# RWKV-7 recurrence feeding a merged four-expert MLP: the order of TensorE's products in a pass, rearranged from the sixth pass on

## The chip, the cores and the metric

The kernel runs on one core of a Trainium2 chip, in fp32. The metric is the device time of one execution in microseconds (us), lower is better; the median of a few executions is compared. Engines are named as in the profile: PE is TensorE's matrix products and PEld its weight loads, DVE is VectorE, ACT is ScalarE, POOL is GpSimd, SP is the engine that issues most DMAs. Each engine works through its own instructions in their order; semaphores connect them.

## The reference

Two stages. The first is a linear recurrence over 768 tokens for 4 x 8 heads of 40 channels. The second takes the 3072 tokens with 320 channels through four experts of hidden size 1024, weighted by normalised domain probabilities.

```python
for t in range(S):                                   # B, H, S, D = 4, 8, 768, 40
    y[:, :, t] = einsum('bhd,bhde->bhe', r_t, state)
    Sa = einsum('bhde,bhe->bhd', state, a_t)
    state = state * w_t[:, :, None, :] - einsum('bhd,bhe->bhde', Sa, b_t) \
            + einsum('bhd,bhe->bhde', v_t, k_t)
x = y.transpose(0, 2, 1, 3).reshape(3072, 320)
p = domain_probs / (domain_probs.sum(-1, keepdims=True) + 1e-9)
for e in range(4):
    out += p[:, e:e+1] * (maximum(x @ w1[e], 0) @ w2[e])
```

## The kernel before, in words

**Units and passes.** Tokens are cut into 12 chunks of 64. A *unit* is one chunk of two batches (128 partitions are 2 x 64 tokens); there are 24 units (`NU`). The main loop (line 1100) has one *pass* per unit u = 1 to 23 and weaves four kinds of work into it: the state step of unit u and u+1 (`step`), the inverse of unit u+1 (`merge`), the work inside unit u+2 and u+3 that needs no state (`within`, `substitute`), and the MLP of chunks already finished (`todo`). All but the MLP are generators; `run(gen, n)` lets n of their parts emit instructions, so the loop's order of calls is the order in which work is emitted. `EARLY` is 5: passes below 5 have one order, the others another. Unit 0 and 1 go through the MLP one by one (`mixture_of_unit`), later units two at a time (`mixture_of_chunk`).

**Two forms of product.** Everything with heads of 40 channels uses a quarter of the array: products of 64 rows by 64 columns (`quadrants`, line 383), four at a time in the four quadrants. The MLP and the transposes use the full 128 x 128. In between stands one case: the input has 320 = 128 + 128 + 64 channels. The first MLP product of a weight piece therefore has a part on the *last* 64 channels, in quadrants (`up_last`, line 751), and a *main* part on 256 channels, in the full form (`up_main`, line 765); both add into the same two PSUM banks (`ph`), the last channels first. I call a run of quadrant products between full ones a *quadrant stretch*, and the other a *full stretch*.

**MLP pieces.** `ups(e, x)` makes half the hidden layer of expert e: last channels, main part, relu on ACT (line 778) into `hs`. `down_1` is one tile of three products of 8 steps (`p431`, 12 matmuls in the program), `down_2` two tiles (`p75`, `p26`, 16 matmuls); they take `w2`, sums of it, and sums of `hs` (`a`, DVE, line 897). Their results are scaled and added into `osb` on DVE (line 791; the first expert's line 789). Half of these adds are 320 wide, half 160. In the trace each such fp32 matmul appears twice: 12 in the program are 24 rows. `piece.lead` emits only the part on the last channels, ahead of its piece, so that it falls in a quadrant stretch. `mix(n)` emits n pieces; a pass takes 8 (two in each `gap`), of which four are ups. `w1` pieces (640 KB) arrive in two buffers, `w1p`; the next load waits until the piece before the last has been used.

**State step.** `step` has for each unit: `prn` (state times A, and the transposed state), RH on DVE (line 654), SN on ACT; `psat`, then SaT and SX copies on ACT; `pxr`, from which DVE makes the masked part of SX (line 400) and ACT the copies RS (line 700); `pdy`, a K term and an N term per quadrant; then Y and the new state on DVE, and Y goes by DMA into xT. The N term needs SX.

**Work inside a unit.** `within`: G (scan of decays, DVE), `pg` (transpose of G, PE), gp (product and reciprocal, DVE), n_tok, k_tok, AT (DVE), VT and RT (32 x 32 transposes on DVE of raw loads), `pNT`, `pKT` (transposes, PE) and copies NT, KT (ACT); `pc` and VC (masked copy, DVE); `pfe` and F (ACT); `pe` and ET (masked copy, DVE); `pev` and EV (ACT). `substitute` inverts the triangular F: blocks (DVE and ACT), M (DVE, line 553) and a long run of small operations on POOL giving Z. `merge`: Qc and QTc (transposes on DVE, lines 604 and 606), `pY`, Yq (ACT), `pQ`, QT (ACT).

**What sets the order.** A scheduler orders the instructions of an engine by its own estimates, except where `tc.keep_in_program_order` pins them. `in_order[0]` pins all products on TensorE; it is on up to u = 5 and off after it. `pin` pins some of `within` for the first units. `q.apart` is set for units from `EARLY + 2`: F is copied before `pe` is made. PSUM has 8 banks: 5 (`big`) for the recurrence, used in turn, 3 (`mm`) for the MLP. A tile that takes over a bank waits until the old contents have been read.

Of the kernel before, what the change touches and what calls it, by code (L numbers as in the profile page):

```python
# [15 lines left out]
def kernel(  # L16
# [42 lines left out]
    P = 128  # L59
# [342 lines left out]
    def within(q):  # L402
# [74 lines left out]
        if q.u > 1:  # L477
            pin(turn_raw(q.AT[:], n["rawA"][:]))
        at_ij = q.AT[:].rearrange("p (i j) t -> p i j t", i=2)
        ins = other.tensor_tensor(out=at_ij, in0=at_ij, in1=Gv.rearrange("p (j i) t -> p i j t", i=2), op=ALU.mult)  # L480
        pin(ins)
# [13 lines left out]
        if q.u == 1 or q.u >= PADDED:  # L495
            causal_scores(VT)
            yield
# [10 lines left out]
        if q.apart:  # L508
            copy_F()
            yield  # L510
# [125 lines left out]
    def step(q, xT):  # L636
# [59 lines left out]
        if not q.start:  # L696
# [10 lines left out]
        pdy = quadrants(  # L707
            banks("pdy"), 0, BY_TOKENS, D + L - lo,
            lambda j, s, i: (i, s, j, q.K[half(i), head(j, s), :], q.VC[half(i), head(j, s), lo:D + L]),
            lambda j, s, i: (i, s, j, q.N[half(i), head(j, s), :], SX[half(i), head(j, s), lo:D + L]),  # L710
        )
# [39 lines left out]
    def up_last(k, xT, n):  # L751

        w1 = pieces[k]
        ph = [ps.tile([P, HF // 2, n], FP32, name="ph", tag="mm", bufs=3) for _ in range(2)]

        for f in range(HF // 2):
            for c in range(2):
                for i in range(2):
                    matmul(
                        out=ph[i][half(c), f, :], lhsT=w1.last[part(i), f, half(c)],  # L760
                        rhs=xT[part(i), 2, :], start=(f == 0), stop=False,
                    )
        return ph

    def up_main(k, xT, n, ph):

        w1 = pieces[k]
        h = sb.tile([P, HF, 2 * P], FP32, name="hs", tag="hs", bufs=3)
        for i in range(2):
            for f in range(HF // 2):  # L770
                for g in range(2):
                    at = i * HF // 2 + f
                    matmul(
                        out=ph[i][:, f, :], lhsT=w1.main[:, g, at * P:(at + 1) * P],
                        rhs=xT[:, g, :], start=False, stop=(g == 1 and f == HF // 2 - 1),
                    )
        for i in range(2):
            nc.scalar.activation(  # L778
                out=h[:, i * HF // 2:(i + 1) * HF // 2, 0:n], in_=ph[i][:], func=ACTF.Relu,
            )  # L780
        return h

# [18 lines left out]
    def mixture_of_unit(q):  # L801
# [3 lines left out]
        def ups(e):  # L805
            ph = []

            def lead():
                if not ph:
                    ph.append(up_last(at + 2 * e, q.xT, P))  # L810

            def piece():
                lead()
                hs[e] = [up_main(at + 2 * e, q.xT, P, ph[0])]
                hs[e].append(up_main(at + 2 * e + 1, q.xT, P, up_last(at + 2 * e + 1, q.xT, P)))
                used(at + 2 * e + 2)
                if q.u == 0 and e + 2 < E:
                    load_w2(e + 2)

            piece.lead = lead  # L820
            return piece
# [44 lines left out]
    def mixture_of_chunk(qs, xT):  # L866
# [4 lines left out]
        def ups(e, x):  # L871
            k, ph = at + 2 * e + x, []

            def lead():
                if not ph:
                    ph.append(up_last(k, xT, 2 * P))

            def piece():
                lead()
                hs[e, x] = up_main(k, xT, 2 * P, ph[0])  # L880
                used(k + 1)

            piece.lead = lead
            return piece
# [96 lines left out]
    def lead():  # L981
        if todo and hasattr(todo[0], "lead"):
            todo[0].lead()

# [115 lines left out]
    for u in range(1, NU):  # L1100
        in_order[0] = u <= EARLY
# [16 lines left out]
        ahead = u + 3 < NU and u in range(EARLY, EARLY + 3)  # L1118
        if ahead:
            go(load_raw(begin(u + 3), "W"))  # L1120
        if early:
            lead()
        run(w_next, 99 if early else 1)
        run(s, 1)
        gap(0)


        if early:
            run(s, 1)
        run(w, 1)  # L1130
        if not early:
            run(w_next)
            run(s)

        if early:
            run(w, 1)
            gap(1, 2 if u + 1 == EARLY else None)
            run(s)
        if u == 1:
            mixture_of_unit(q)  # L1140
        elif q.bp:
            mixture_of_chunk(units[u - 1:u + 1], chunks_x[q.c])
        if not early:
            begin_later(len(later))
            run(w, 1)
            run(m, 1)
            gap(1)

        if u + 3 < NU:
            go(load_raw(units[u + 3] if ahead else begin(u + 3), "A" if ahead else "WA"))  # L1150
            load(units[u + 3], "WBKV")
            later.extend(load_raw(units[u + 3], "VR"))
        run(w, 2)

        soon = u in (2, 3, 4)
        if soon:
            run(w, 1)
        if early:
            run(m, 1)
        else:  # L1160
            run(s_next, 1)
            run(m, 1)
        if soon:
            substitute(units[u + 2], nc.gpsimd)
        gap(2)

        if not early:
            run(m, 1)
        if not soon:
            run(w, 1)  # L1170
        if not early:
            lead()
            run(s_next, 1)
        if not soon and u + 2 < NU:
            substitute(units[u + 2], nc.gpsimd)
        if early:
            run(w, 1)
        if u + 3 < NU:
            ws.append(within(units[u + 3]))
            run(ws[u + 3], 1)  # L1180
        if early:
# [5 lines left out]
        else:  # L1187
            gap(3)
        s = s_next
    mix(len(todo))  # L1190
# [30 lines left out]
```

## Time and profile before

| | |
|---|---|
| median of 3 runs | 1103.84 us (1103.26 to 1104.54) |
| the profiled execution, its own time | 1102.3 us |
| its span, first to last instruction | 1100.6 us |
| mean granted TensorE clock | 0.991 |
| DMA moved | 122.18 MB, mean 111 GB/s |
| DVE, ACT, POOL busy, 246.33 to 932.28 us | 498.88, 230.03, 348.26 of 685.95 us |

The stretch from 246.33 to 932.28 us holds passes 6 to 21, which repeat; before it lie the first units, after it the last two units and the rest of the MLP. Busy times of PE are modelled from starts, and products overlap, so an idle time of PE is shown only where a gap is longer than a product; the starts in the timeline tell more. A line's times are the start, the length, and at the end, in brackets, the idle time of the engine before it and what ended it. "x32" is how many instructions were merged into the row.

### The profile page before, as it was taken

To read this page: it belongs to the slowest core of one execution; us is meant where nothing else is said; L and a number is where in the kernel's file an instruction comes from. 1 tells how busy PE (TensorE), PEld (TensorE's weight loads), DVE (VectorE), ACT (ScalarE), POOL (GpSimd) and SP (SyncE) were. 2 spreads that over 40 slices of the span, in tenths; PEclk is the share of its full clock that TensorE was granted. 3 is DMA by queue.
4 is the path that set the end of the run, shared out by engine and by line. 5 is a ranking of instruction groups with operands and counts; after the bars stand their busy time and mean duration, and the time that the engine had idled before them with its cause. 6 is when DMAs were issued, how large, how long until landed. Compare 5 with 4: busy or idle time off the path is not lost.

```text
span 1100.6 us, 38528 instructions
## 1 busy us (share of the span) xinstructions
PE 1070.0 (97%) x16102; PEld 955.8 (87%) x16102; DVE 756.6 (69%) x1551; ACT 353.0 (32%) x956; POOL 502.9 (46%) x1274
## 2 busy tenths in 40 slices
PE   6799899999999999999999999999999999999998
PEld 6677788789998999898999989989998989988887
DVE  7766668887777776767767768767767677543343
ACT  2432444223233233243233242332332432321110
POOL 5106677753463653743734635636537437430000
PEclk9799999999999999999999999999999999999999
DMA  7776545425345363354353444443552532222320
GB/s 117 226 247 138 136 103 117 119 55 136 98 111 127 98 140 97 94 146 103 93 144 94 102 121 104 116 120 84 127 123 65 147 85 67 98 69 82 104 76 13
DMA packets 268868, 122.18 MB, mean 111 GB/s; under 512 B 213736, under 2 KB 242072, under 8 KB 268696
## 3 DMA queue, kind: packets, MB, share of 16 engines
q1 hardware_dynamic: 265416, 119.12, 43.0%
q8 instruction: 127, 2.08, 0.8%
q10 hardware_dynamic: 3280, 0.61, 0.3%
q14 instruction: 45, 0.37, 0.1%
HBM read 111.79 MB, written 3.93 MB: 105 GB/s over the span
## 4 chain that ended last, share of the span: by engine, by line
PE 81%; DVE 7%; POOL 5%; ACT 3%; issue 2%; DMA 1%; SPq 0%; ACTq 0%; DVEq 0%; POOLq 0%
PE ph L76 35%; PE p L76 28%; POOL Z L593 3%; PE pdy L76 3%; PE psat L76 2%; PE pxr L76 2%; POOL Z L580 2%; PE prn L76 1%; PE pfe L76 1%; PE pQ L76 1%; PE po L76 1%; PE pc L76 1%; DVE Z L590 1%; PE pY L76 1%; DVE M L553 1%
## 5 line engine op out<-in xcount | busy, mean ns | idle before, releaser
L76 PE MATMUL ph<-xT,w1p 128*128 128x256 f32 (+3 forms) x3040 | 446.3, 377 | 4.0 <-issue 3.9
L76 PEld LDWEIGHTS ph<-xT,w1p 64*64 64x64 f32 (+1 forms) x3040 | 338.5, 162 | 72.7 <-issue 29.0
L593 POOL TENSOR_TENSOR Z<-Z 128x31 f32<-128x31 f32 (+7 forms) x704 | 260.0, 369 | 55.2
L897 DVE TENSOR_TENSOR a<-hs 128x512 f32<-128x512 f32 x220 | 151.8, 707 | 104.7 <-ACT hs L778 104.7
L580 POOL TENSOR_TENSOR Z<-M,Z 128x62 f32<-128x62 f32 (+7 forms) x352 | 144.1, 409 | 132.3 <-DVE M L569 106.4
L778 ACT ACTIVATE hs<-ph 128x512 f32<-128x512 f32 (+1 forms) x208 | 115.3, 564 | 226.5 <-PE ph L76 225.4
L76 PE MATMUL p<-sums,a 128*128 128x160 f32 x1056 | 164.9, 299 | 0.0
L76 PEld LDWEIGHTS p<-sums,a 128*128 128x128 f32 x1056 | 152.8, 190 | 2.2
L791 DVE SCALAR_TENSOR_TENSOR osb<-p,gate,osb 128x320 f32<-128x320 f32 (+1 forms) x243 | 108.1, 481 | 57.8 <-PE p L76 53.6
L550 POOL COPY below<-F 32x256 f32<-32x256 f32 x48 | 22.8, 475 | 198.7 <-ACT F L506 197.0
L76 PE MATMUL p<-w,a 128*128 128x160 f32 x704 | 105.9, 301 | 0.2 <-ACT hs L778 0.2
L76 PE MATMUL p<-w,hs 128*128 128x160 f32 x704 | 102.9, 299 | 0.0
L76 PEld LDWEIGHTS p<-w,hs 128*128 128x128 f32 x704 | 100.2, 190 | 2.2
L76 PEld LDWEIGHTS p<-w,a 128*128 128x128 f32 x704 | 98.3, 190 | 3.0 <-ACT hs L778 3.0
L612 POOL COPY QT<-QTc 32x256 f32<-32x256 f32 x96 | 51.7, 539 | 76.9 <-DVE QTc L606 67.7
L553 DVE STREAM_TRANSPOSE M<-blocks 128x1024 f32<-128x1024 f32 x24 | 47.4, 1977 | 38.1 <-ACT blocks L547 37.9
L700 ACT COPY RS<-pxr 64x256 f32<-64x256 f32 x88 | 32.2, 366 | 105.2 <-DVE SX L400 43.1
L451 DVE RECIPROCAL gp<-gp 128x320 f32<-128x320 f32 x24 | 51.6, 2151 | 0.7
L535 ACT COPY EV<-pev 64x160 f32<-64x160 f32 x96 | 23.1, 286 | 89.7 <-PE pev L76 89.3
L604 DVE STREAM_TRANSPOSE Qc<-Z 128x256 f32<-128x256 f32 x24 | 15.0, 627 | 46.2 <-POOL Z L593 46.1
L627 ACT COPY QT<-pQ 32x128 f32<-32x128 f32 x96 | 24.6, 256 | 59.9 <-PE pQ L76 58.2
L659 ACT COPY SN<-prn 128x256 f32<-128x256 f32 x44 | 14.9, 372 | 78.6 <-DVE RH L654 78.6
(149 smaller groups left out, 1357.5 us busy)
## 6 DMA issues: line engine op xcount, KB each, us to landing
w1p<-in_moe_w_dram SPq DMA_DIRECT2D x95, 512.0 KB
w1p<-in_moe_w_dram SPq DMA_DIRECT2D x190, 64.0 KB
w<-in_moe_w_dram SPq DMA_DIRECT2D x4, 1280.0 KB
sums<-in_moe_w_dram SPq DMA_DIRECT2D x9, 512.0 KB
natW<-in_w_dram SPq DMA_DIRECT2D x48, 80.0 KB
natB<-in_b_dram SPq DMA_DIRECT2D x48, 80.0 KB
natK<-in_k_dram SPq DMA_DIRECT2D x48, 80.0 KB
out_dram<-osb SPq DMA_DIRECT2D x46, 80.0 KB
```

The source lines that it names most:

```text
L76: return stated(nc.tensor.matmul(**k))
L451: pin(nc.vector.reciprocal(out=gp[:], in_=gp[:]))
L535: nc.scalar.copy(out=of_slot(q.EV[half(p)], i ^ p)[:, :, 0:D], in_=pev[i][half(p)])
L553: ins = nc.vector.transpose(out=M[:], in_=cols)
L580: ins = eng.tensor_tensor(out=Z[:, 1:3, 0:n, j + 1:Q], in0=M[:, j:j + 2, None, j + 1:Q].to_broadcast([P, 2, n, m]), in1=Z[:, here, 0:n, j: ...
L593: eng.tensor_tensor(out=z[:, 0], in0=z[:, 0], in1=z[:, x], op=ALU.add)
L612: ins = nc.gpsimd.tensor_copy(out=q.QT[quarter(i), :, quarter(i % 2)], in_=QTc[quarter(i)])
L627: nc.scalar.copy(out=of_slot(to[quarter(2 * r)], y), in_=src)
L700: nc.scalar.copy(out=RS[half(s), x ^ s::2], in_=prs[x][half(s)].rearrange("p (j i) t -> p j i t", i=2),)
L778: nc.scalar.activation(out=h[:, i * HF // 2:(i + 1) * HF // 2, 0:n], in_=ph[i][:], func=ACTF.Relu,)
L791: nc.vector.scalar_tensor_tensor(out=to, in0=p, scalar=sc, in1=to, op0=ALU.mult, op1=ALU.add)
L897: nc.vector.tensor_tensor(out=t[:], in0=x, in1=y, op=op)
```

## The change

From pass 5 on, the loop body is written anew, and three things follow from it.

1. The order on TensorE is pinned in all passes, and a pass has three quadrant stretches in place of four: (1) last channels of one piece, `prn`, `pY`, `pfe`, last channels of the next; (2) `pQ`, `pc`, `pe`, last channels, `psat`; (3) `pxr`, `pev`, last channels, `pdy`. Between (3) and the next (1) lies one long full stretch: `pg`, a main part, `p75` and `p26`, a second main part, `pNT`, `pKT`, `p431`.
2. One first product of a pass begins with its main part and ends with its last channels (`begin`, `end`), so that its last channels can stand in the next quadrant stretch. The second product of each expert of units 0 and 1 does so too. For this the first product is a class, `Up`, in place of closures.
3. `pdy` makes all K terms, yields, and then all N terms, from pass 5 on (the start flag then clears a quadrant of a bank at its first K term only).

Also `pc` is made after F is copied for units from 7 on, AT is pinned for them, and weight sums, loads and leads are placed in the new body by hand.

```diff
-            pin(turn_raw(q.AT[:], n["rawA"][:]))
+            pin(turn_raw(q.AT[:], n["rawA"][:]), q.apart)
         at_ij = q.AT[:].rearrange("p (i j) t -> p i j t", i=2)
         ins = other.tensor_tensor(out=at_ij, in0=at_ij, in1=Gv.rearrange("p (j i) t -> p i j t", i=2), op=ALU.mult)
-        pin(ins)
+        pin(ins, q.apart)
...
-        if q.u == 1 or q.u >= PADDED:
+        if q.u == 1 or (q.u >= PADDED and not q.apart):
...
         if q.apart:
             copy_F()
+            yield
+            causal_scores(VT)
             yield
...
-        pdy = quadrants(
-            banks("pdy"), 0, BY_TOKENS, D + L - lo,
-            lambda j, s, i: (i, s, j, q.K[half(i), head(j, s), :], q.VC[half(i), head(j, s), lo:D + L]),
-            lambda j, s, i: (i, s, j, q.N[half(i), head(j, s), :], SX[half(i), head(j, s), lo:D + L]),
-        )
+
+        def of_K(j, s, i):
+            return i, s, j, q.K[half(i), head(j, s), :], q.VC[half(i), head(j, s), lo:D + L]
+
+        def of_N(j, s, i):
+            return i, s, j, q.N[half(i), head(j, s), :], SX[half(i), head(j, s), lo:D + L]
+
+        if q.u < EARLY:
+            pdy = quadrants(banks("pdy"), 0, BY_TOKENS, D + L - lo, of_K, of_N)
+        else:
+            p = banks("pdy")
+            for term, opens in ((of_K, True), (of_N, False)):
+                for j, s, i in BY_TOKENS:
+                    row, col, at, lhsT, rhs = term(j, s, i)
+                    matmul(
+                        out=p[row][half(col), at * (D + L - lo):(at + 1) * (D + L - lo)], lhsT=lhsT, rhs=rhs,
+                        start=(opens and j == 0), stop=(not opens and j == NJ - 1),
+                    )
+                if opens:
+                    yield
+            pdy = [by(x[:, 0:NJ * (D + L - lo)], D + L - lo) for x in p]
...
+    class Up:
+
+        def __init__(self, k, xT, n, done):
+            self.at, self.n, self.done, self.ph = (k, xT), n, done, None
+
+        def lead(self):
+            if self.ph is None:
+                self.ph = up_banks(self.n)
+                up_last(*self.at, self.ph, True)
+
+        def __call__(self):
+            self.lead()
+            up_main(*self.at, self.ph, False)
+            self.done(positive(self.n, self.ph))
+
+        def begin(self):
+            self.ph = up_banks(self.n)
+            up_main(*self.at, self.ph, True)
+
+        def end(self):
+            up_last(*self.at, self.ph, False)
+            self.done(positive(self.n, self.ph))
...
             def piece():
-                lead()
-                hs[e] = [up_main(at + 2 * e, q.xT, P, ph[0])]
-                hs[e].append(up_main(at + 2 * e + 1, q.xT, P, up_last(at + 2 * e + 1, q.xT, P)))
+                a()
+                b.begin()
+                b.end()
                 used(at + 2 * e + 2)
                 if q.u == 0 and e + 2 < E:
                     load_w2(e + 2)
 
-            piece.lead = lead
+            piece.lead = a.lead
...
+    def open_next():
+        if not todo:
+            return None
+        piece = todo.pop(0)
+        piece.begin()
+        return piece
...
-        in_order[0] = u <= EARLY
+        in_order[0] = True
...
+        ahead = u + 3 < NU and u < EARLY + 3
+        if ahead:
+            go(load_raw(begin(u + 3), "W"))
+        if u == EARLY:
+            run(w_next)
+            lead()
+        run(s, 1)
+        run(w_next)
+        lead()
+        run(s)
+        run(sum_ops, sums_at.get(4 * u, 0))
+        run(w, 1)
+        mix(2)
+        if q.bp:
+            mixture_of_chunk(units[u - 1:u + 1], chunks_x[q.c])
+        begin_later(len(later))
+        run(w, 1)
+        run(m, 1)
+        run(sum_ops, sums_at.get(4 * u + 1, 0))
+        up = open_next()
+        run(w, 1)
+        mix(1)
+        if u + 3 < NU:
+            go(load_raw(units[u + 3] if ahead else begin(u + 3), "A" if ahead else "WA"))
+            load(units[u + 3], "WBKV")
+            later.extend(load_raw(units[u + 3], "VR"))
+
+        if up:
+            up.end()
+        run(s_next, 1)
+        run(m, 1)
+        run(w, 1)
+        lead()
+        if u + 2 < NU:
+            substitute(units[u + 2], nc.gpsimd)
+        run(sum_ops, sums_at.get(4 * u + 2, 0))
+        mix(2)
+
+        run(m, 1)
+        run(w, 2)
+        lead()
+        run(s_next, 1)
+        if u + 3 < NU:
+            ws.append(within(units[u + 3]))
+            run(ws[u + 3], 1)
+        todo[:2] = todo[1::-1]
+        mix(2)
         s = s_next
-    mix(len(todo))
+    while todo:
+        mix(2)
+        up = open_next()
+        mix(1)
+        if up:
+            up.end()
+            lead()
```

`up_last` and `up_main` take the banks and a flag that says which of them opens the sum; `positive` is the relu part of the old `up_main`. Passes below 5 keep their order. The old loop body for passes from 5 on, which this replaces, is in the listing above.

## The prediction

> **What bounds the kernel now.** I read four views. First the page: engine shares, and the chain that ended last.
>
> ```profile
> PE 1070.0 (97%) x16102; PEld 955.8 (87%) x16102; DVE 756.6 (69%) x1551; ACT 353.0 (32%) x956; POOL 502.9 (46%) x1274
> ...
> PE 81%; DVE 7%; POOL 5%; ACT 3%; issue 2%; DMA 1%; SPq 0%; ACTq 0%; DVEq 0%; POOLq 0%
> ```
>
> TensorE (PE) is nearly always busy and carries 81% of the chain. Next, TensorE's own waits from 246 to 932 us, which are the sixteen passes 6 to 21, and the sum of that stretch (us; busy PE, PEld, DVE, ACT, POOL; clock; DMA share; GB/s):
>
> ```profile
> PE pc L76 <- DVE RT L241: 0.9, 1, 0.9
> PE ph L76 <- issue: 0.5, 1, 0.5
> PE p L76 <- ACT hs L778: 0.2, 1, 0.2
> ...
> 246.33:932.28 685.95, 685.23 (x10688) 621.82 (x10689) 498.88 (x1006) 230.03 (x623) 348.26 (x880) 1.00 0.44 110
> ```
>
> A pass takes 685.95/16 = 42.87 us, at full clock, with almost no visible idle time. What can be saved is therefore hidden in the spacing of products. So third, a timeline of TensorE over one pair of stretches in a pass (start, us, what):
>
> ```profile
> 560.93 3.72 PE L76 MATMUL ph<-xT,w1p 128*128 128x256 f32 x16
> 564.49 2.34 PE L76 MATMUL p<-w,hs 128*128 128x160 f32 x16
> 566.66 1.25 PE L76 MATMUL p<-sums,a 128*128 128x160 f32 x8
> 567.84 0.69 PE L76 MATMUL pe<-AT,KT 64*64 64x64 f32 x32
> 568.36 0.65 PE L76 MATMUL pxr<-RT,SaT 64*64 64x64 f32 x32
> 568.82 0.65 PE L76 MATMUL pxr<-RT,SN 64*64 64x64 f32 x32
> 569.29 4.74 PE L76 MATMUL ph<-xT,w1p 64*64 64x256 f32 x32
> 573.87 1.25 PE L76 MATMUL p<-sums,a 128*128 128x160 f32 x8
> ```
>
> Read the differences of starts. Sixteen p take 566.66-564.49 = 2.17, so 0.136 each; the next eight should take 1.09 and take 1.18: 0.09 us are lost where the form goes from 128x128 to 64x64. Full ph products follow one another every 0.216 us (a look at 561.25 to 564.49 has fifteen spacings in 3.24), so sixteen need 3.46 and take 3.56: 0.10 lost on the first. The mixed row of 32 ph takes 573.87-569.29 = 4.58; without the full half's 3.56, the sixteen 64-row products take 1.02, where four at a time every 0.216 would be 0.86: 0.16 lost on leaving the form. One quadrant stretch thus costs 0.09+0.10+0.16 = 0.35 us in changes alone. A pass has four, the new one three.
>
> **The change, part by part.** The sum is made against the profiled execution (1102.3 us; span 1100.6, 1.7 around it) and then moved to the median of the three runs, 1103.84, which lies 1.5 above it.
>
> *Fewer changes of form.* Reading the two programs' orders of products, stretches of either form fall from 241 to 183: 29 quadrant stretches fewer. Twenty-one are late (passes 5 to 23 one each, the tail of the last chunk two): 21 x 0.35 = -7.4. Eight lie in the products of the first two units, where the chain passes through POOL's Z and DMA landings; there a stretch gained is often waited away. All kept is -2.8, none 0; I take half, -1.4.
>
> *Waits that go.* One pass, 546.85 to 589.60 (pc to pc), takes 42.75 and holds one visible stall: sixteen p<-w,a take 554.38 to 556.82 = 2.44 instead of 2.17. Without it 42.48, so the mean pass loses 0.39 in such gaps. They are p26 waiting for relu on ACT (ACT stands in SN behind DVE's RH), and psat waiting for the QT copies of pQ. In the new order ACT has F and two blocks copies, 1.5 us, before the relu, but p26 comes some 3 us after that; and psat has pc, pe and ph (1.8 us) behind pQ instead of pfe and ph (1.3), against 1.1 for the copies and about 0.25 of latency. Kept ends: 0 to 17 x 0.39 = -6.6; I take -6.0, since both have cover in numbers.
>
> *K part first.* Today K and N terms alternate on the same quadrant. The 64 pdy take 1.48 us (536.49 to 537.97); 16 groups every 0.089 (two K starts of one quadrant, 536.61 and 536.70) would be 1.42. A gain of 0.06 to 0.15 with the smoother exit; 0.1 x 18 = -1.8. That K part is also the cover for the next item.
>
> *A new wait in the third stretch.* pxr, pev, ph, pdy now stand in one stretch. pdy's second bank is the bank of pxr0, so it waits for one SX copy on DVE and two RS copies on ACT. RS rows:
>
> ```profile
> 570.59 1.50 ACT L700 COPY RS<-pxr 64x256 f32<-64x256 f32 x4 [5.30 <-DVE SX L400]
> ```
>
> That is 0.37 a copy. pxr ends 0.98 after the stretch begins, its last result some 0.2 later; SX0 0.43, RS 0.75: 2.4. TensorE arrives after pxr 0.98, pev 0.47, ph 0.86: 2.3. Wait 0.1; x 17 = +1.7. The N part needs SX1 at about 2.1 and comes at 3.1. Ends: 0, and 0.8 if pdy had to wait until both banks are empty (SX1 to 2.1, RS of the second bank to 3.1); I take 0.1, since only the first bank is asked for.
> [...]
>
> *A new wait for QTc.* This is the large one. DVE works in order. At the end of the long full stretch the new program has, in every second pass (eight of them), two osb adds on p431, then RT, Qc, osb, QTc; pY stands behind QTc. Before, pc and prn (1.45 us) stood ahead of pY and in most passes QTc ahead of the adds. Prices:
>
> ```profile
> 549.64 1.01 DVE L789 TENSOR_SCALAR osb<-p,gate 128x320 f32<-128x320 f32 x2
> 550.56 0.67 DVE L791 SCALAR_TENSOR_TENSOR osb<-p,gate,osb 128x160 f32<-128x160 f32 x2
> ...
> 582.36 0.65 DVE L241 STREAM_TRANSPOSE RT<-rawR 128x512 f32<-128x512 f32 x1
> 582.94 0.71 DVE L715 TENSOR_TENSOR Y<-pdy,RS 128x256 f32<-128x256 f32 x2
> ...
> 589.41 0.41 DVE L241 STREAM_TRANSPOSE G<-rawW 128x256 f32<-128x256 f32 x1
> 589.74 0.40 DVE L606 STREAM_TRANSPOSE QTc<-Qc 128x256 f32<-128x256 f32 x1
> ```
>
> With 0 at the first quadrant product: p431's result at 0.1, two adds 0.92, RT 0.58, Qc 0.49 (588.92 to 589.41), half add 0.30, QTc 0.40: 2.8. TensorE is there after ph 0.86+0.05 and prn 0.93: 1.85. It waits 0.95, say 1.0 with the semaphore; everything behind pY on TensorE waits too. 8 x 1.0 = +8.0. In the other passes QTc precedes the adds: ready at 0.5, no wait. It would cost nothing if p431 were read later (then 0); the upper end is 1.3.
>
> *Pass 5.* There all four adds (1.5), two RH (0.55, after prn) and RT, Qc stand ahead of QTc: about 4.2 against 1.9, +2.3. Five weight sums (0.85 each) also lie on DVE, two of them before and three behind M: VC's copy of pc comes near 18.1, psat at 16.4: +1.7, taken 1.5. Gone is the wait of pNT for n_tok (1.3 in the waits of the first 246 us; 1.0 taken), since pNT now lies 12 us behind pg. Together +2.8, ends 0 and +5.
>
> *DMA.* The 64-row half of one product moves 8 us on, and so its w1p buffer is freed later; its successor is then needed 12 us after that. Issues of 1.6 us and about 5 us of transfer fit. rawV's eight issues now stand on SP behind a w1p load; VT may be up to 1.5 us late on DVE, with 3 us to spare before p431's adds are needed. Taken as nothing; without that cover DVE's SX comes late and pdy with it.
>
> Sum: -7.4 -1.4 -6.0 -1.8 +1.7 +8.0 +2.8 = -4.1. 1102.3-4.1 = 1098.2 profiled; 1103.84-4.1 = **1099.7 us**.
>
> **Rivals.**
> - *QTc is not late* (DVE or p431 shift so that pY finds it): the +8.0 goes, 1091.7. For it: Z is done some 10 us before (POOL's 22 us begin when M is ready). Against it: the order on DVE is fixed and p431's end opens it. Chance 0.10.
> - *The waits only move* (the 0.39 a pass stays, as another copy is last): -4.1+6.0 = +1.9 at the full amount, 1105.7; half of it 1102.7. No clear sign. Chance 0.19 for ending within 0.2%, about what this kernel's measurement can tell from none.
> - *Slower: psat waits for VC on DVE.* psat's second bank is freed by the VC copy of pc, which now stands behind M and the whole run of hs sums and adds. Count one undelayed pass from its first quadrant product. TensorE: stretch 1 3.8, full stretch 8.0, pQ, pc, pe and ph 2.3: psat at 14.1. ACT: two relus to 2.3, two SN and four Yq (0.33 and 0.20 apart) to 3.75, two F 0.65: 4.4, two blocks 0.8: 5.2. DVE: M, its square and sum 3.6 (563.56 to 567.15): 8.85; two sums 1.25: 10.1; then osb, sum, half, sum, osb, sum, half at 0.47, 0.61 and 0.30 apart, 3.4: 13.5; VC 0.43: 13.9. 0.2 us are to spare. Each further 0.1 on DVE costs 1.7 over 17 passes; from 0.6 more than counted (0.4 late per pass, +6.8) the kernel is slower: 1106.5; with 0.6 late 1110. For it: DVE is busy 498.88 of 685.95 us, 73%, and this run has no gap. Against it: the prices are rows with POOL at work beside them. Chance 0.23.
> - *The change does not do what it says* is excluded by the order of products.
>
> **How the numbers follow.** Forecast 0.48, of its own range 1094 to 1101.6; with the first rival 0.58 for faster by over 0.2% (below 1101.6), 0.19 within, 0.23 above 1106. The range 1091 to 1109 takes in QTc's end of 0 and VC 0.5 late.
>
> **What would show it.** Pass length 42.1 in passes with QTc early and 43.1 in the others; three quadrant stretches with 0.35 each; pY as a TensorE wait on DVE QTc of about 1.0, eight times; psat free of QT. Wrong if psat or pdy wait on VC, SX or RS by more than 0.3, or if passes are equal in length.

## The result, and the profile after

The changed kernel takes 1167.61 us (median of 5, 1164.20 to 1170.72) against 1103.84 before: a ratio of 1.0579 (1.0562 to 1.0596; here and below the ratio to the kernel before, measured beside it, with its 95% interval). The forecast was 1099.7. The profiled execution has a span of 1167.5 us, 66.9 more than before. First its page, engine shares and the chain that ended last, by engine and by line:

```profile
PE 1082.7 (93%) x16102; PEld 971.3 (83%) x16102; DVE 747.0 (64%) x1551; ACT 354.4 (30%) x956; POOL 487.9 (42%) x1274
...
PE 61%; SPq 18%; DVE 12%; issue 4%; DMA 4%; ACT 1%; DVEq 0%; ACTq 0%
PE ph L76 26%; PE p L76 19%; SPq L762 10%; PE pdy L76 3%; SPq L223 3%; SPq L300 2%; DMA rawR<-in_r_dram 2%; PE psat L76 2%; PE pxr L76 2%; SPq L840 2%; PE pfe L76 1%; PE pY L76 1%; PE pQ L76 1%; PE po L76 1%; PE pc L76 1%
```

TensorE's part of the chain falls from 81% to 61%, and SP's issuing of DMAs, 0% before, is 18%: line 762 (Y into xT), 223 (raw loads), 300 (w1p) and 840 (stores). The view of TensorE's waits, passes 5 to 22 (us in total, times, longest), says what TensorE stood for; "issue" means that the profile shows nothing it waited for:

```profile
PE pY L76 <- DVE QTc L608: 37.8, 16, 5.4
PE pdy L76 <- issue: 7.1, 5, 2.5
...
PE psat L76 <- DVE VC L400: 1.2, 1, 1.2
```

pY waits for QTc, as forecast, but for 37.8 us in place of 8. The starts show it in every pass: ahead of pY 0.8 to 1.4 us are lost in one half of the passes and 2.7 to 5.6 in the other, the passes in which a finished chunk is stored. One of the latter, first SP's queue, then DVE, then TensorE (start, us, what):

```profile
656.64 9.25 SPq L762 DMA_DIRECT2D xT<-Y  x12
665.99 1.66 SPq L300 DMA_DIRECT2D w1p<-in_moe_w_dram  x3
667.70 1.53 SPq L223 DMA_DIRECT2D rawR<-in_r_dram  x3
669.33 2.45 SPq L840 DMA_DIRECT2D out_dram<-osb  x4
671.82 1.61 SPq L223 DMA_DIRECT2D rawR<-in_r_dram  x1
```
```profile
674.39 0.55 DVE L833 TENSOR_SCALAR osb<-p,gate 128x320 f32<-128x320 f32 x1 [1.68 <-DMA out_dram<-osb]
674.86 0.70 DVE L241 STREAM_TRANSPOSE RT<-rawR 128x512 f32<-128x512 f32 x1
675.48 0.57 DVE L606 STREAM_TRANSPOSE Qc<-Z 128x256 f32<-128x256 f32 x1
...
676.15 0.41 DVE L608 STREAM_TRANSPOSE QTc<-Qc 128x256 f32<-128x256 f32 x1
```
```profile
672.27 0.67 PE L76 MATMUL prn<-ident,state 64*64 64x64 f32 x32
676.71 0.59 PE L76 MATMUL pY<-QTc,below 64*64 64x64 f32 x13 [3.77 <-DVE QTc L608]
```

SP begins the last rawR transfer 15 us after Y was ready: twelve issues into xT (0.77 each), three of w1p, three of rawR and four stores stand ahead. RT needs that transfer, Qc and QTc stand behind RT on DVE, pY behind QTc. The stores share the delay: in the pass shown DVE's osb waits for an older store (the 1.68 us in brackets) and RT follows without a gap of its own; in the passes without a store RT itself stands 2.7 to 3.3 us. The kernel before had this order at the same place:

```profile
575.65 2.02 SPq L223 DMA_DIRECT2D rawR<-in_r_dram  x4
580.28 1.31 SPq L202 DMA_DIRECT2D natW<-in_w_dram  x2
581.70 1.35 SPq L202 DMA_DIRECT2D natV<-in_v_dram  x2
584.63 9.58 SPq L744 DMA_DIRECT2D xT<-Y  x12
594.31 1.66 SPq L300 DMA_DIRECT2D w1p<-in_moe_w_dram  x3
```

rawR goes ahead of Y. The transfers still in `later`, and the stores, are begun inside the first `mix` of a pass. The old body called that (`gap(0)`) ahead of `run(s)`, which begins Y's transfers; the new one calls `mix(2)` behind it. So whatever the first pieces of a pass begin has moved past twelve issues. A lower granted clock comes on top: behind this wait it is 0.50 for 3.41 us (us; then busy PE, PEld, DVE, ACT, POOL; clock; DMA share; GB/s):

```profile
672.50:676.70 4.20, 0.44 (x32) 0.32 (x23) 2.52 (x7) 0.65 (x2) 0.00 (x1) 1.00 0.41 82
677.59:681.00 3.41, 3.41 (x35) 2.32 (x27) 1.37 (x3) 2.58 (x9) 2.11 (x5) 0.50 0.78 175
```

From pass 5 on to pass 22 the clock stands at 0.50 for 30.7 us in sum, in seven stretches of 3.41 or 6.83 us; in the kernel before it never does there. In the stretch shown, two full ph products start 0.43 us apart (680.20 and 680.63), where the prediction read 0.216 at 1.00. So, as an estimate from these numbers, at most half of the 30.7, some 15 us, is lost by it.

From the prn of pass 5 to that of pass 22 the seventeen passes take 788.5 us against 725.9, so 62.6 of the 66.9 lie there; 1.1 lie ahead, 3.2 behind. Against the shortest length of each stretch in these kernels, the first quadrant stretch of a pass is over by some 54 us in sum (waits for QTc and the clock behind them), the second by 7, the third by 9.

### The profile page after: what moved, and what is told of

It reads as the page before. It is cut to its first block, busy times and chain, and to the rows that moved or that the text cites. A ratio compares the mean times of both kernels' runs of the same rounds, so it can differ in the third digit from the quotient of the medians.

```text
span 1167.5 us, 38490 instructions
## 1 busy us (share of the span) xinstructions
PE 1082.7 (93%) x16102; PEld 971.3 (83%) x16102; DVE 747.0 (64%) x1551; ACT 354.4 (30%) x956; POOL 487.9 (42%) x1274
## 4 chain that ended last, share of the span: by engine, by line
PE 61%; SPq 18%; DVE 12%; issue 4%; DMA 4%; ACT 1%; DVEq 0%; ACTq 0%
PE ph L76 26%; PE p L76 19%; SPq L762 10%; PE pdy L76 3%; SPq L223 3%; SPq L300 2%; DMA rawR<-in_r_dram 2%; PE psat L76 2%; PE pxr L76 2%; SPq L840 2%; PE pfe L76 1%; PE pY L76 1%; PE pQ L76 1%; PE po L76 1%; PE pc L76 1%
## 5 line engine op out<-in xcount | busy, mean ns | idle before, releaser
L76 PE MATMUL ph<-xT,w1p 64*64 64x256 f32 (+3 forms) x3040 | 449.3, 385 | 6.2 <-PE ph L76 2.8
L76 PEld LDWEIGHTS ph<-xT,w1p 128*128 128x128 f32 (+1 forms) x3040 | 341.8, 165 | 65.8 <-issue 16.3
L595 POOL TENSOR_TENSOR Z<-Z 128x31 f32<-128x31 f32 (+7 forms) x704 | 241.2, 343 | 55.2
L582 POOL TENSOR_TENSOR Z<-M,Z 128x62 f32<-128x62 f32 (+7 forms) x352 | 160.6, 456 | 95.3 <-DVE M L571 69.5
L614 POOL COPY QT<-QTc 32x256 f32<-32x256 f32 x96 | 40.5, 422 | 331.3 <-DVE QTc L608 327.6
L400 DVE COPY_PREDICATED SX<-mask_up,pxr 128x256 f32<-128x256 int32 x48 | 18.8, 442 | 60.2 <-PE pxr L76 60.2
L733 DVE TENSOR_TENSOR Y<-pdy,RS 128x256 f32<-128x256 f32 x44 | 16.7, 420 | 61.8 <-PE pdy L76 60.6
L457 ACT COPY NT<-pNT 128x512 f32<-128x512 f32 x24 | 14.1, 586 | 136.3 <-PE pNT L79 136.0
L76 PE MATMUL pY<-QTc,below 64*64 64x64 f32 x384 | 18.2, 240 | 37.8 <-DVE QTc L608 37.8
L76 PEld LDWEIGHTS pY<-QTc,below 64*64 64x64 f32 x384 | 15.4, 150 | 40.6 <-issue 39.7
```

The costliest lines, as they stand in the source:

```text
L76: return stated(nc.tensor.matmul(**k))
L582: ins = eng.tensor_tensor(out=Z[:, 1:3, 0:n, j + 1:Q], in0=M[:, j:j + 2, None, j + 1:Q].to_broadcast([P, 2, n, m]), in1=Z[:, here, 0:n, j: ...
L595: eng.tensor_tensor(out=z[:, 0], in0=z[:, 0], in1=z[:, x], op=ALU.add)
L614: ins = nc.gpsimd.tensor_copy(out=q.QT[quarter(i), :, quarter(i % 2)], in_=QTc[quarter(i)])
```

## The experiments

Lines marked + are added to the changed kernel, or to the kernel named; lines marked - are taken out. The passes' sum is always from the prn of pass 5 to that of pass 22 (before 725.9, changed 788.5).

**raw_first**

```diff
+        begin_later(len(later))
         if u == EARLY:
```


> The changed kernel with one line more: the transfers of raw r and v that are still to be begun are begun at the head of each late pass, so the last four of raw r stand on SP ahead of the twelve transfers of Y into xT and not behind them. Theory Q (SP's queue: RT, and with it Qc and QTc, waits for the last rawR transfer): TensorE's waits for QTc, 37.8 us in the changed kernel, fall below 5 us; the excess of the stretch with pY, 54 us over 17 passes, goes almost whole; the time falls from 1167.6 to between 1095 and 1112. Rival S (the three-stretch order itself is too tight: pY comes too early for Z and QTc whatever the queue does): waits for QTc stay above 25 us, the time above 1150. Rival T (TensorE's lower granted clock, 0.974 against 0.991, is the cause and not a consequence): the time stays above 1150 and the clock at 0.97; Q expects 0.99.

1124.3 us, ratio 1.0190 (1.0162 to 1.0218). The waits for QTc fall from 37.8 to 0.2 us and the passes' sum to 749.6: one line takes back 43 of the 64 us, 39 of them in the passes. S and T fall. On DVE, RT, Qc and QTc now stand ahead of p431's adds:

```profile
551.82 0.68 DVE L241 STREAM_TRANSPOSE RT<-rawR 128x512 f32<-128x512 f32 x1
...
552.98 0.63 DVE L606 STREAM_TRANSPOSE Qc<-Z 128x256 f32<-128x256 f32 x1
...
553.78 0.41 DVE L608 STREAM_TRANSPOSE QTc<-Qc 128x256 f32<-128x256 f32 x1
...
559.03 0.55 DVE L833 TENSOR_SCALAR osb<-p,gate 128x320 f32<-128x320 f32 x1 [2.58 <-PE prn L76]
```

Six of the seventeen passes now last 42.25 or 42.26 us, below the 42.87 of before (mean; its shortest is 42.70). But the time is 12 us above Q's range, and the clock, 0.980 to 0.986, below the 0.99 that Q expects, so more is wrong than rawR.

**raw_first_mixed** (raw_first, with pdy's products of K and N mixed again)

```diff
-        if q.u < EARLY:
+        if True:
```


> The kernel with the loads at the head of the pass, and pdy's K and N terms mixed again as before the change. The prediction priced K part first at 0.1 us in each of 18 passes, and its cover for SX at some 0.7 us more: 1.8 to 14 us slower than the kernel with the loads at the head of the pass. If K first is worth nothing: the same within 1 us.

1125.7 us, ratio 1.0212 (1.0171 to 1.0253) against 1.0190: the intervals overlap, and 0.1 us in each of 17 passes would be lost in them. vt_held and vt_mixed below are the quieter pair.

**raw_on_act**

```diff
+        go(later, nc.scalar)
+        del later[:]
         mix(2)
```


> The changed kernel, in which the transfers of raw r that are left at the long full stretch are begun by ACT and not by SP, at the same place of the program. If it is the queue (Q), the order of products and the place in the program don't matter: time within 6 us of the kernel that begins them at the head of the pass, 1095 to 1115, QTc waits below 5 us. If it is the place of the loads in the program, or the three-stretch order itself (S): above 1150. Four issues on ACT in place of SP may cost ACT up to 4 x 0.6 = 2.4 us a pass ahead of its copies; if those are then late, the time is 5 to 40 us above the other.

1175.3 us, ratio 1.0643 (1.0607 to 1.0680): a miss. The waits of this kernel:

```profile
DVE RT L241 <- DMA rawR<-in_r_dram: 73.0, 16, 5.5
...
PE ph L76 <- DVE osb L835: 36.4, 16, 3.0
```

ACT began its four transfers a pass ahead, as soon as RT had read the buffer. The scheduler put RT on DVE ahead of Y and osb, while three more rawR transfers still stood on SP behind a w1p load that waits for ph. So DVE stood still ahead of everything, and ph waited for osb. So the place of RT on DVE moves with its transfers, and a late one hurt in either place.

**before_late** (the kernel before, with its last four rawR transfers begun behind `run(s)`)

```diff
+        held = [] if early else later[:]
+        if held:
+            del later[:]
         gap(0)
...
             run(s)
+            later.extend(held)
+            begin_later(len(later))
```


> The kernel before, with nothing of the change, but the last four raw r transfers of each late pass begun behind the twelve transfers of Y into xT (they were begun ahead of them). Theory Q: RT then comes some 9 us later on SP (twelve issues at 0.77 us) against a slack of about 4 us (last issue at 577.7, RT at 582.4), so each of 17 passes grows by 3 to 9 us: 1150 to 1250, with TensorE waiting for RT (pc) or QTc (pY). Rival S: the old order of products has room, so the time stays within 1100 to 1115.

1214.5 us, ratio 1.0983 (1.0942 to 1.1023), with none of the change's products moved. Its waits of TensorE in the passes have one line:

```profile
PE pc L76 <- DVE RT L241: 76.4, 17, 8.4
```

This move alone, put into the old order, costs 111 us. Together with raw_first it shows the cause: where those four transfers stand on SP.

**raw_then_store**

```diff
+        begin_later(len(later))
         mix(2)
```


> The changed kernel; the four raw r transfers that are left stay behind the twelve transfers of Y into xT, but stand ahead of the w1p load and of the four stores of osb that follow. Theory Q (every issue ahead of the last rawR costs SP's time): in the passes with stores rawR is begun some 1.7 + 2.5 = 4 us earlier, in the others 1.7; of TensorE's gaps ahead of pY (0.8 to 1.4 in one half of the passes, 2.7 to 5.6 in the other) the first vanish and the second fall to about 0 to 1.5: 17 passes give back 25 to 40 us, 1125 to 1143. The stores, still behind, go on stopping DVE's osb, which the rawR wait covered: up to 8 x 2 of it comes back, so rather 1130 to 1145. If the twelve issues alone set the wait: the same as the changed kernel, 1165.

1147.9 us, ratio 1.0414 (1.0375 to 1.0454): seven issues fewer ahead of the last rawR give 20 us. That is some 3 us above the range with the stores. The other 23 of raw_first's 43 us go with the twelve issues of Y, so the rest of the queue counts nearly as much.

**raw_store_act** (raw_first, and)

```diff
-        for i, eng in enumerate((nc.sync, second)):
+        for i, eng in enumerate((nc.sync, second) if q.u < 2 or todo == [] else (nc.scalar, nc.scalar)):
```


> The kernel with rawR at the head of the pass (1124.3), and the four stores of osb of each chunk begun by ACT, which is idle there, and not by SP behind Y's transfers. Theory: what is left over the kernel before comes mostly from the stores: DVE's first osb of a chunk waits until the stores of the chunk before the last have read their tile (16.7 us of DVE waits in 11 cases), and p431's bank, RH, SN and the next ph wait behind it; TensorE's gaps at ph of 1.2 to 2.6 us in six even passes, with the clock lost after them, make 12 to 16 us. Expected 1108 to 1113. Rival: these gaps are late instructions (issue), not the stores; then 1122 to 1126.

1117.5 us, ratio 1.0134 (1.0095 to 1.0172): 7 us less, half of what was expected. What the stores did in raw_first:

```profile
823.92 1.01 DVE L833 TENSOR_SCALAR osb<-p,gate 128x320 f32<-128x320 f32 x2 [4.16 <-DMA out_dram<-osb]
824.84 0.67 DVE L835 SCALAR_TENSOR_TENSOR osb<-p,gate,osb 128x160 f32<-128x160 f32 x2
825.42 0.55 DVE L656 TENSOR_TENSOR RH<-prn,EV 128x160 f32<-128x160 f32 x2
```

The first osb of a chunk waits until the older chunk's store, issued at 819.24 behind Y, has read its tile. RH stands behind it, and so does ph, whose bank it frees: TensorE had a gap of 2.64 us up to 825.61. (Gaps here and below are from start to start.) With the stores on ACT one such gap over 0.9 us is left of five, and DVE's waits for stores fall from 16.7 to 7.0 us; passes 5 and 6 (49.1 and 46.9 us) and single gaps remain.

**raw_store_act_sums** (three weight sums go from pass 5 to pass 6; in this kernel they come after their first use, so a part of one chunk's last expert is made from the older sums)

```diff
-    sums_at.update({4 * 4 + 3: 2, 4 * 5 + 0: 3, 4 * 5 + 1: 2, 4 * 5 + 2: 3})
+    sums_at.update({4 * 4 + 3: 2, 4 * 5 + 0: 3, 4 * 5 + 1: 2, 4 * 6 + 0: 3})
```


> As the kernel with stores on ACT, and the last three weight sums on DVE go from the sixth pass (behind M, ahead of VC) to the start of the seventh pass. The prediction gave the sixth pass +2.8 us of waits (QTc behind adds, VC behind sums); in the kernel with rawR first the pass takes 49.7 from prn to prn against 42.75 before. Expected 2 to 6 us less than with the sums in place: 1104 to 1110.

1112.1 us, ratio 1.0077 (1.0051 to 1.0103), 5.5 less: passes 5 and 6 fall to 45.4 and 45.2. The later kernels have the three sums in pass 4.

**raw_store_act_units** (in `mixture_of_unit`, `b()` for `b.begin()` and `b.end()`)

> As the kernel with stores on ACT, but the second product of each expert of units 0 and 1 begins with its last channels again, as before the change (14 stretches of either form more at the start). The prediction gave this part of the change -1.4 us: so 1.4 us slower than the kernel with stores on ACT, between 0 and 2.8.

1119.4 us, ratio 1.0133 (1.0104 to 1.0162), no different from 1.0134. The prn of pass 5 starts at 243.7 against 244.8 us. Kernels with one and the same start spread by 5 us there (242.6 to 247.9), so the 1.4 us can be neither shown nor excluded.

**r_on_act_pinned** (raw_store_act with the sums in pass 4 and the last chunk as before the change, and)

```diff
+            for move in load_raw(units[u + 3], "R"):
+                tc.keep_in_program_order(move(nc.scalar))
...
+                    pin(turn_raw(t[:], n["raw" + x][:]), q.apart and x == "R")
```


> The kernel with stores on ACT, and four edits more: all eight raw r transfers of a unit are begun by ACT in the stretch where it waits for pQ, none by SP; RT is held behind AT on DVE, with Qc and QTc behind it and p431's adds after them; three weight sums go from the sixth pass to the fifth; the rest of the MLP after the last pass has its first products in the order of before. Theory Q: with SP 8 issues lighter and nothing of DVE behind a late transfer, the passes are equal, at 42.25 us (the length of the undisturbed passes of the kernels with rawR first, floor 42.05), against 42.87 before: 17 x 0.62 = 10.5 us less than before, of which the sixth pass and some instruction waits take 3 to 6 back; the tail gives back the 3.1 us that it lost. Expected 1093 to 1103, below the kernel before (1104.1). Rival: the three-stretch order has uneven waits of its own whatever the queues do: 1107 to 1117.

1159.7 us, ratio 1.0513 (1.0490 to 1.0537): a miss again. pY has no wait left in any pass, but:

```profile
ACT hs L806 <- DMA rawR<-in_r_dram: 62.8, 12, 7.0
...
PE p L76 <- ACT hs L806: 29.5, 14, 4.2
```

Eight issues ahead of a relu hold ACT up to 7 us, and p waits for that relu. One case, ACT's queue and ACT:

```profile
482.59 0.32 ACTq L223 DMA_DIRECT2D rawR<-in_r_dram  x1
...
483.01 7.18 ACTq L223 DMA_DIRECT2D rawR<-in_r_dram  x7
490.25 1.08 ACT L806 ACTIVATE hs<-ph 128x512 f32<-128x512 f32 x2 [6.85 <-DMA rawR<-in_r_dram]
```

The issues alone take 3.1 to 4.5 us a pass. The rest is a wait: the fourth rawR of this case stood from 484.15 to 487.84 us, after a w1p load that SP had begun at 482.31; that it waited for this load is the author's reading, which the lines above don't show. The relu starts at 490.25, 0.06 us after the last of the seven issues (483.01 + 7.18), so the loss was moved from SP to ACT.

**qtc_behind_adds** (r_on_act_pinned with `run(m, 1)`, which makes Qc and QTc, behind the `mix(1)` that makes p431)

> As the last, but Qc and QTc stand behind all four of p431's adds on DVE in every late pass, with raw r on time. This is by itself the wait that the prediction priced at 1.0 us for two adds, Qc, half an add and QTc in eight passes. By the same working: p431's result 0.1 after the stretch begins, four adds 1.5, Qc 0.49, QTc 0.40 = 2.5; TensorE arrives at 1.85: 0.65 to 0.75 in each of 17 passes, 11 to 13 us more than the kernel without it, with gaps ahead of pY of 0.7 and no more. If the whole loss of the changed kernel had been this wait: 40 us or more.

```profile
PE pY L76 <- DVE QTc L615: 12.6, 15, 0.8
```

0.84 us in each of 15 passes: the wait that the prediction priced exists at about its price. What it costs in time isn't shown: the whole, 1153.1 us, ratio 1.0454 (1.0425 to 1.0483), lies below r_on_act_pinned and not 11 to 13 above, as both kernels lose most on ACT, and differently.

**loads_early** (rawV and rawR by SP, both begun behind `up.end()`; stores on ACT, RT held, sums and last chunk as in the last two)

```diff
         if up:
             up.end()
+        begin_later(len(later))
```


> As the kernel with raw r on ACT and RT pinned, but all of raw v and raw r go by SP again, begun together at the start of the pass's first full stretch, right behind the w1p load that the last channels set free: about 8 us of issues, done some 20 us ahead of RT and ahead of the twelve transfers of Y. ACT issues none but the stores. Theory Q (transfers begun late on a queue that works in order, and an engine that stands still behind them, are the whole loss; ACT's relu behind eight issues was the loss of the last kernel): pY without a wait, passes of 42.25 us, the whole 1093 to 1103 and so not above the kernel before. Rival U: the next w1p loads, now 8 us later on SP, become late for the first products of the long full stretch: gaps of 1 to 4 us at ph there, 1105 to 1130.

1115.4 us, ratio 1.0104 (1.0083 to 1.0125). pY is free, U's gaps at ph don't come, but no pass lasts less than 42.85. DVE in one pass:

```profile
735.50 0.71 DVE L241 STREAM_TRANSPOSE VT<-rawV 128x512 f32<-128x512 f32 x1 [1.69 <-DMA rawR<-in_r_dram]
...
737.45 0.77 DVE L400 COPY_PREDICATED VC<-mask_up,pc 128x256 f32<-128x256 int32 x2
```

With rawV early the scheduler puts VT ahead of VC, and psat waits for VC: 0.6 us in every pass, and 1.4 to 2.5 where a raw load is late.

**vt_held** and **vt_mixed** (loads_early with VT held behind the adds of the long full stretch; and that with K and N mixed)

```diff
-                    pin(turn_raw(t[:], n["raw" + x][:]), q.apart and x == "R")
+                    pin(turn_raw(t[:], n["raw" + x][:]), q.apart)
```


> As the kernel with raw v and r begun early, but VT is held on DVE behind the adds of the long full stretch, so that VC, which frees psat's second bank, has no VT and no late raw v ahead of it. Theory V (the prediction's slower rival: VC on DVE has 0.2 us to spare, VT's 0.65 in front of it costs what goes beyond): the excess of the second quadrant stretch falls from 1.19 to 0.4 to 0.6, passes from 42.86 to 42.1 to 42.3, the four passes with gaps of 1.4 to 2.5 us at psat lose them; 17 x 0.65 + 5 = 16 us less: 1098 to 1106. Rival: the three-stretch order waits elsewhere in that stretch (QT, the next w1p): 1112 to 1116.

> As the last, with pdy's K and N terms mixed as before the change. K part first saved 1.3 us with raw r first (not clear of noise) and cost 3.7 in the kernel before. By the prediction 1.8 us slower than the last; by the run on the kernel before up to 3.7 faster; an instruction that comes late in the K-first run (pdy after 28 to 31 of 32 N products, 1 to 2 us, in some three passes) would then be missing or elsewhere.

1103.8 us, ratio 0.9993 (0.9981 to 1.0006), and 1105.5, ratio 1.0008 (0.9997 to 1.0019). Undisturbed passes are 42.27 and 42.36: the third quadrant stretch takes 4.06 us with K first and 4.16 mixed, the 0.1 that the prediction took. But vt_held's sum is 732.3 (vt_mixed's 728.7), not 17 x 42.27 = 718.6: pass 5 is longer, and a few passes hold gaps without a semaphore. TensorE in one of them:

```profile
612.62 0.95 PE L76 MATMUL pdy<-SX,n_tok 64*64 64x104 f32 x30
615.29 0.30 PE L76 MATMUL pdy<-SX,n_tok 64*64 64x104 f32 x1 [1.72 <-issue]
615.52 0.66 PE L79 MATMUL pg<-ident,G 128*128 128x128 f32 x4
```

One product of 32 comes 2 us late. vt_held's page counts the transfers of instructions (packets, MB, share):

```profile
q8 instruction: 127, 2.08, 0.7%
```

That is 16 KB each, and 32,588 instructions of TensorE (16,102 products, as many weight loads, 384 semaphores) over 127 are 257; one transfer for every 256 is an estimate from these. Counting TensorE's instructions up to each gap over 0.9 us that ends without a semaphore, from pass 6 on, in blocks of 256:

```
changed    38.75  75.76  112.76  117.75
raw_first  38.75  75.76  96.76  112.75  117.75
vt_held    38.75  59.75  75.76  112.75  117.75
vt_mixed   75.76  112.75  117.75
```

The same instructions, in kernels with different waits. The transfers agree: vt_held's five gaps end 1.4 to 1.5 us after the last byte of a 16 KB transfer on queue 8, begun 2.4 to 2.5 us before the gap's end. The kernel before has no such gap in its passes.

**vt_shift** (vt_held with `keep_warm(32)` and `keep_warm(26)` for 16 and 10)

> As vt_held, with 32 more warm-up products on TensorE in the first 20 us, where it waits: 128 more of its instructions, half a block of 256. Theory I (TensorE's instructions come in blocks of 256, 16 KB each, one transfer on queue 8 per block; where the end of a loaded block falls in the last part of the third quadrant stretch, the next block is not there yet): the gaps at pdy and ph near 313, 484, 613, 914 and 956 us of vt_held go, and new ones of 1 to 2 us come where the block now ends late in pdy: in the passes whose pdy lies near 399, 699 and 870 us (perhaps 570), again at an instruction count of x.75. The time stays within 3 us of vt_held. Rival W (pdy waits for SX, a bank or a transfer, in passes that have something else in common): the gaps stay in the same passes, near 313, 484, 613, 914, 956.

The gaps at 313, 484, 613, 914 and 956 us are gone, and new ones stand at 49.76, 65.76 and 86.75 blocks: two in the passes named (pdy near 399 and 699 us of vt_held), one, of 1.2 us, in a pass that was not; none came near 870. In the pass that had lost 2 us, and in one that had lost nothing:

```profile
622.81 0.96 PE L76 MATMUL pdy<-SX,n_tok 64*64 64x104 f32 x31
623.70 0.55 PE L79 MATMUL pg<-ident,G 128*128 128x128 f32 x3
```
```profile
408.97 0.61 PE L76 MATMUL pdy<-SX,n_tok 64*64 64x104 f32 x17
410.38 0.58 PE L76 MATMUL pdy<-SX,n_tok 64*64 64x104 f32 x14 [0.80 <-issue]
```

W falls; I holds for the counts, though not every pass where it named a gap has one. The passes' sum is 723.6, 8.8 less. The time is 1107.2, ratio 1.0032 (1.0017 to 1.0046), a little outside the 3 us: the start is 10.7 us longer.

**vt_fewer** (`keep_warm(4)`, `(2)`, `(0)` for 16, 10, 12) and **vt_small** (32 more of 8 columns)

> As vt_held, with 32 warm-up products fewer on TensorE at the start (128 instructions less, half a block; the result does not use them). Theory I: gaps at the same instruction counts modulo a block, so in the same passes as with 32 more (near 399 and 699 us, small near 870), and the passes from the sixth to the last prn take 723 to 726 us against 732.4 in vt_held; nothing lost at the start unless a colder clock costs 1 to 3 us there. 1094 to 1100, below the kernel before. Rival: the 8.8 us shorter passes of vt_shift were chance, and the time is that of vt_held, 1102 to 1106.

> As vt_held, with 32 more warm-up products of only 8 columns, put where TensorE waits for n_tok at the start: the same half block, at 64 x 0.05 = 3 us at most. Theory I: as vt_fewer, 1095 to 1101. Rival: 1102 to 1106.

The passes' sums are 721.9 and 722.3, as expected; the times are not: 1103.9, ratio 1.0006 (0.9992 to 1.0021), and 1113.5, 1.0072 (1.0049 to 1.0096). The first prn starts at 113.0 us in vt_held, 119.0 here with fewer products and 127.8 with narrow ones. Why fewer lengthen the start too is open.

**vt_fill** (vt_held, and in pass 5, where TensorE waits for n_tok, 32 quadrant products that nothing reads)

```diff
+        if u == EARLY:
+            for _ in range(2):
+                quadrants(banks("fill"), 0, BY_TOKENS, L, lambda j, s, i: (
+                    i, s, j, ident[half(i), 0:L], ident[half(i), 0:L],
+                ))
         run(w, 1)
         mix(1)
```


> As vt_held, with 32 products of 64 x 64 in the four quadrants (128 instructions, half a block, about 1 us) in the sixth pass, where TensorE waits 1.8 us for n_tok ahead of pNT; nothing reads them. Start as in vt_held. Theory I: gaps at pdy in the passes near 399 and 699 us only, passes from the sixth to the last prn 723 to 726 us against 732.4 in vt_held: 1095 to 1099, faster than the kernel before by 0.4 to 0.8%. Rival: the whole stays at 1102 to 1106, as the start's spread or other waits take it.

1099.4 us, ratio 0.9952 (0.9940 to 0.9964): faster than the kernel before, the passes' sum 723.4. TensorE's waits in the passes, all that is left:

```profile
PE ph L76 <- issue: 2.5, 2, 1.4
PE ph L76 <- DMA w1p<-in_moe_w_dram: 1.2, 1, 1.2
PE pdy L76 <- issue: 0.8, 1, 0.8
PE psat L76 <- DVE VC L400: 0.2, 1, 0.2
```

The gap at pdy lies at 400 us, as expected; near 699 us only 0.4 us is lost, and one of 1.1 us at ph, at 65.75 blocks, was not named. That the time meets the prediction's 1099.7 is chance: it takes all these edits to the changed kernel, and terms that the prediction's sum does not have.

## Why the prediction was wrong, step by step

- **DMA: the step that failed.** "Taken as nothing" spoke of w1p and of rawV's eight issues. The last four of rawR and the four stores, which the first `mix` of a pass begins, were not followed past Y's twelve. The term put at nothing measured 43 us for rawR alone (raw_first), and 7 more for the stores (raw_store_act).
- **A new wait for QTc: a symptom taken for the cause.** In every second pass RT, Qc and QTc stood behind p431's adds because of the late rawR: in raw_first, nothing else changed, they stand ahead of the adds in every pass after pass 5. (That the scheduler reckons with the landing is the reading of this.) The forecast was 8.0 us, the changed kernel's waits 37.8. The working was sound for what it priced (0.84 measured where 0.7 is worked out for four adds), but the place of RT on DVE should have led to its transfer. The first rival, "that pY finds it", was set back by "the order on DVE is fixed", without asking what had fixed it.
- **Form changes, waits that go, K first, SX.** By the prediction a pass becomes 0.35 + 0.35 + 0.1 - 0.1 = 0.70 shorter; the mean pass of before, 42.87, became an undisturbed one of 42.27, 0.60 less. From the shortest of before, 42.70, it is 0.43, and no run takes the items apart. K first is 0.1 in the third stretch, as taken, in the new order; in the kernel before it alone gave 1107.1, ratio 1.0034 (1.0021 to 1.0047); its expectation stands at the end of this section. SX costs nothing: no wait of pdy for it is seen in vt_held. Some 0.2 us a pass stays in the second stretch (3.57 us against 3.36 in the best), which no row puts to a name.
- **Pass 5.** +2.8 was taken. In the changed kernel its two waits came at about their prices: pY stood 2.35 us (2.3 taken), psat 1.2 for VC (1.5 taken). What it left out shows in raw_first, where the pass lasts 49.7: ph stands another 2.65 us, until DVE's osb add, behind the weight sums, is done. Three sums moved away take 3.6 us off it (raw_store_act_sums against raw_store_act); in vt_held it is still 2.2 over 42.27. Pass 6 there is 2.2 over too, mostly by the late instruction at 315 us.
- **The first units and the last chunk.** Of the -1.4 nothing shows. The last chunk lost 3.2: its joined stretches, with no prn and pY in between, stand four times 1.08 us from one ph to the next; r_on_act_pinned and its followers have the old order there, and some 2 of the 3.2 us are back.
- **The rival with VC** was the nearest miss of the right kind: its slack was as small as counted (VT's 0.65 ahead of VC costs 0.6 a pass), but in the changed kernel it did not decide.

K first alone, in the kernel before (**before_k_first**: the changed kernel's pdy block, from pass 5 on):

> The kernel before with K part first alone (no other edit). The prediction gave 0.1 us a pass in 18 passes: 1.8 us less than before, between 1.1 and 2.7; nothing if N's wait for SX took it back.

The profiled span is 3.6 us longer. 1.3 us of it lie ahead of the prn of pass 5, where nothing was edited, and 2.2 in the passes, of which two gaps of 1 us ahead of ph, against one of 0.5 before, make up 1.5. So its sign in the old order isn't the forecast one; whether K first brings these gaps is open.

## What to carry to other kernels

When a loop body is rearranged, follow every DMA that a moved call begins, also those hidden in a helper's list of things still to begin, and ask for each queue what it has been moved past. An engine's order that looks odd (a transpose behind adds) may be the scheduler's answer to a late transfer: look at that transfer before pricing the order. And count a queue of small transfers as time on the engine that issues them: here twelve took SP 9.2 us, and eight took ACT 3.1 to 4.5, or up to 7 with a wait among them.

## What the runs showed of the hardware

- Twelve issues of 4 to 20 KB take SP 9.2 us, 0.77 each (changed kernel). Four transfers behind those twelve, and what else stood there, cost the 43 us between it and raw_first. Eight issues ahead of ACT's relu take 3.1 to 4.5 us, and with a wait among them ACT stands up to 7.0 (r_on_act_pinned).
- TensorE's gaps of 0.8 to 2.5 us without a semaphore stand in a dense stretch or just behind it (176 products in some 4 us), at x.75 or x.76 blocks of 256 of its instructions, and end 1.2 to 1.6 us after the last byte of one of the 127 transfers of 16 KB on queue 8. With 128 more instructions ahead (vt_shift) they are gone from where they were and stand in other passes. Why the kernel before has none in its passes is not shown.
- At or behind seven of TensorE's waits in the changed kernel's passes, of 2.48 to 5.35 us, the granted clock was 0.50 for 3.41 us or twice that, 30.7 us in sum; at others, of 3.00, 2.47 and 2.35 us, it stayed at 1.00. In before_late it was 0.50 for 78.5 us, in the passes of the kernel before never.
